# Fifteen pairs and a plain last group: reordering the second layer of a Strassen/Winograd mixture of experts

## The chip, the cores and the metric

The kernel runs on one core of one Trainium2 chip. The metric is the device time in microseconds of one execution; a kernel's time is the median of its runs. Engines are named as in the profile: PE is TensorE (matmul), DVE is VectorE, ACT is ScalarE, POOL is GpSimd, SP is SyncE, whose queue issues all the transfers told of here.

## The reference

```python
def _attn_ref(q, k, v, n_global, n_local):          # q, k, v: 4 x 8 x 768 x 64
    scores = (1 / sqrt(D)) * q @ k^T
    keep = (pos_k < n_global) | ((rel >= 0) & (rel < n_local))   # 8 global, 96 local
    ... # ALiBi-like bias, mask, softmax with + 1e-9 under the sum
    return a @ v

def _moe_ref(x, w_gate, w1, w2):                     # x: 3072 x 512, 8 experts, F = 1024
    P = exp(logits - max)
    for _ in range(8):                               # Sinkhorn
        P /= P.sum(1) + 1e-9;  P /= P.sum(0) + 1e-9;  P *= N / E
    for e in range(8):
        out += P[:, e:e + 1] * (relu(x @ w1[e]) @ w2[e])
```

The attention's output is the input `x` of the mixture; every token goes through every expert.

## The kernel before, in words

Attention runs first, in 8 units of 384 tokens, with a part of expert 0 as filler. Then comes the mixture. All of it is in float32 accuracy: each operand is split into a high part and a rest, and each product is three matmuls (high by rest, rest by high, high by high).

The 3072 tokens are three passes of 1024 (8 tiles of 128). The hidden units that are left are 31 groups (`NG`) of 256 (two tiles of 128): three of expert 0, four of each other expert. The first layer of a group and a pass is Strassen's scheme: seven products m1 to m7, each six matmuls of 128x512, into four PSUM banks a, b, c, d; DVE adds the banks up, and the relu makes four blocks h11, h12, h21, h22.

- **Pass 0** (it works on the last 1024 tokens) prepares each group's weights as it goes: `strassen_stage` loads them (`w1f`, `w2f`) and forms their sums on POOL, `strassen_pair` splits all into high and rest (`split`: ACT casts the high part, POOL subtracts), `spill_weights` writes them to DRAM together with the Winograd sums of w2 (`winograd_blocks`). The second layer of this pass is plain: `second` runs `layer2` tile by tile into `y_ps` and adds into `acc` on DVE. For the first group of expert 1 (g = 3) it scales each of the eight `acc` tiles with the gate first, on ACT (L1175, `first_scaled`). At the head of the pass, `reload_first` fetches the first layer's operands of tokens spilled earlier, the m-operands (`op_m`, tiles named x_... or m_... in the order).
- **Passes 1 and 2** read the prepared weights back (`wb`, a ring of five slots; `load_blocks`, issued two items of the plan ahead). `layer1_scaled` is the first layer; the relu is multiplied by the gate (L750), and the seven operands p1 to p7 of the Winograd scheme are h-blocks or sums of them: POOL forms the sums d7, d5, d6, d4 and all the rests (in an order that is kept), ACT the high parts. `second_layer` runs seven products of six matmuls a group in the order p3, p7, p5, p1, p6, p4, p2, accumulates a chunk of groups in PSUM (`c_acc`) and adds it into `sums` in SBUF: ACT copies it for the first chunk (L1272), DVE adds it for others (L1275). The chunks are (0), (1,2), ..., (29,30). Products p6, p4, p2 of a chunk run after the first half of the next group's first layer.
- **At a pass's end** the last chunk runs whole ("end"). The JOIN additions (L1280, on DVE and two on POOL) make the blocks of the output from the seven sums, `turned` transposes them tile by tile (four 128x128 transposes into one bank `o_t`), and one DVE operation (L1247) adds the pass's seed (expert 0's filler part from attention, `ys`) times the gate; a DMA writes the tile. For pass 1 this is put off until group 0 of pass 2 has its first layer; in pass 2 half of it stands ahead of product p2 and half at the end.

After each product of group 30 in pass 1, `used` reloads that product's operands for pass 2. PE's order is the program's through passes 1 and 2; POOL's is within `layer1_scaled`, SP's and ACT's is at the head of pass 0; elsewhere a scheduler places instructions within each engine. Every DMA of SP waits in its queue for what it needs, and for the landing of the DMA eight before it.

Of the kernel before, what the change touches and what calls it, by code (L numbers as in the profile page):

```python
# [17 lines left out]
P = 128  # L18
# [549 lines left out]
class Moe:  # L568
# [73 lines left out]
    def strassen_pair(self, staged, pool):  # L642

        KH = self.KH
        s, a11, a22, w2f = staged
        w1 = pool.tile([P, 7, 2, KH * P], F32R, name="w1")
        w2 = pool.tile([P, 2, FG, self.DM], F32R, name="w2")

        def cols(a):
            return a.rearrange("p (k c) -> p k c", c=P)  # L650

        self.split(cols(w1[:, 0, 0]), cols(w1[:, 0, 1]), a11)
        self.split(cols(w1[:, 6, 0]), cols(w1[:, 6, 1]), a22)
        self.split(w2[:, 0], w2[:, 1], w2f)
        self.split(w1[:, 1:6, 0], w1[:, 1:6, 1], s.rearrange("p n k c -> p n (k c)"))
        return w1, w2, w2f
# [74 lines left out]

    def layer1_scaled(self, x, blocks, share, full, ops, tmp, ps, tag, waits, used):

# [3 lines left out]
        bank = {n: ps.tile([P, WIDE], F32, name=f"bank_{n}", tag=tag) for n in "cdab"}  # L737
        base = self.block_products(bank, x, blocks)

        def product(m, *args):  # L740
# [13 lines left out]

        def rest(k, src):
            gp(out=ops[k][:, 1], in0=src, in1=ops[k][:, 0], op=ALU.subtract)

# [11 lines left out]
        tt(out=t3, in0=t3, in1=c, op=ALU.subtract)  # L769
        high("p3", h12)  # L770
        gp(out=d7, in0=h12, in1=h22, op=ALU.subtract)
        rest("p3", h12)
        high("p7", d7)
# [7 lines left out]
        if waits:  # L781
            rest("p1", h21)
        product("m7", "a", False, True)
# [8 lines left out]
        gp(out=d4, in0=d6, in1=h11, op=ALU.subtract)  # L792
        rest("p6", d6)
        high("p4", d4)
        high("p2", h11)
        rest("p4", d4)
        rest("p2", h11)

# [116 lines left out]
def pipeline(tc, attention, ident, moe, acc, scratch):  # L915
# [12 lines left out]
    with ExitStack() as top:  # L928
# [154 lines left out]

        reload_first(("m1", "m6", "m3"))
        staged = moe.strassen_stage(*groups[1], stage, sync)
        reload_first(("m4", "m7"))
        for _ in moe.gate(NU - 1, xs[NU - 1], sps, "s", sps, "s"):
# [26 lines left out]
        def spill_weights(g):  # L1114

            w = wts[g]
            t = moe.winograd_blocks(w, w2pool)
            to = w_spill[g] = dram.tile([P, 14, 2, FULL], F32R, name=f"ws{g}")
            dma(to[:, 0:7], w[0])
            dma(to[:, 10], w[1][:, :, 1, 0:FULL])  # L1120
            for d in range(2):
                dma(to[:, 12 + d], w[1][:, :, 0, d * FULL:(d + 1) * FULL])
            dma(to[:, 7:10], t[:, 0:3])
            dma(to[:, 11], t[:, 3])
# [35 lines left out]
        def second(g, hs):  # L1160
            e, b = groups[g][0], passes[0]
            first_scaled = e != 0 and groups[g - 1][0] == 0
            for i in range(2):
                for t in range(WT):
# [6 lines left out]
                    if e == 0:  # L1171
                        nc.vector.tensor_tensor(out=a, in0=y_ps, in1=a, op=ALU.add)
                    else:
                        if first_scaled:
                            nc.scalar.mul(a, a, moe.pm[:, tt, 0:1])  # L1175
                        nc.vector.scalar_tensor_tensor(out=a, in0=y_ps, scalar=moe.pm[:, tt, e:e + 1], in1=a,  # L1176
                                                       op0=ALU.mult, op1=ALU.add)
# [36 lines left out]
        held = [acc[:, j] for j in range(BT)] + [scratch[:, n * WIDE:(n + 1) * WIDE] for n in (2, 3, 4)] + extra  # L1214
        sums = {k: held[2 * n:2 * n + 2] for n, k in enumerate(SECOND_ORDER)}
        moe.pe = attention.pe

        def load_blocks(g, layer, part):
            base, (lo, hi) = 7 * layer, ((0, SPLIT), (SPLIT, 7))[part]
            t = wring.tile([P, SPLIT, 2, FULL], F32R, name="wb")  # L1220
            dma(t[:, 0:hi - lo], w_spill[g][:, base + lo:base + hi])
            for n in range(lo, hi):
                blocks_of[g, layer, n] = t[:, n - lo]

        def first_layer(p, g):
# [8 lines left out]
            return moe.layer1_scaled(ops, lambda i: blocks_of[g, 0, i], share, full, ops_of[g % 2], tmp, mps, "h",  # L1234
                                     g % 2 == 1, used)

        def turned(p, i, seeds):
            outs = sums["p1"] + sums["p6"] if i else list(tmp) + sums["p5"]
            for t in range(WT):
                j = 2 * t + i  # L1240
                tt = passes[p] * BT + j
                o_ps = cps.tile([P, DM], F32, name="o_t", tag="c")
# [4 lines left out]
                nc.vector.scalar_tensor_tensor(out=outs[t], in0=seeds[j], scalar=moe.pm[:, tt, 0:1], in1=o_ps,  # L1247
# [7 lines left out]

        def second_layer(gs, order, ends=False, amid=None):
            begins = gs[0] == 0
            for k in order:
                if amid and k == "p2":
                    amid()  # L1260
                n = SECOND_BLOCKS.index(k)
# [19 lines left out]

        chunks_of = [(0,)] + [(g, g + 1) for g in range(1, NG, 2)]

# [6 lines left out]
        def plan(p):  # L1290

            behind = ()
            for gs in chunks_of:
# [7 lines left out]
                else:  # L1301
                    yield "second", gs, SECOND_ORDER[0:SPLIT]
                    behind = gs

        def loads(what, x, y):
            if what == "first":
                return [(y, 0, 0), (y, 0, 1)]
            if what == "end":
                return [(g, 1, part) for part in range(2) for g in y]
# [3 lines left out]
        for y in loads(*todo[1]):  # L1313
            load_blocks(*y)
        finish = None
        for n, (what, x, y) in enumerate(todo):
            if what == "first":
                rest = first_layer(x, y)
                next(rest)
                if n + 1 < len(todo) and todo[n + 1][2] == SECOND_ORDER[SPLIT:]:  # L1320
                    second_layer(*todo[n + 1][1:])
                next(rest, None)
                if finish:
                    finish()
                    finish = None
            elif what == "second":
                if y != SECOND_ORDER[SPLIT:]:
                    second_layer(x, y)
            elif x + 1 < NB:
                second_layer(y, SECOND_ORDER, True)  # L1330
                seeds = load_seeds(x, [ops_of[y[0] % 2][k][:, s].bitcast(F32) for k in SECOND_ORDER for s in range(2)])

                def finish(p=x, seeds=seeds):
                    for i in (1, 0):
                        turned(p, i, seeds)
            else:
                seeds = load_seeds(x, [a.rearrange("p t k c -> p (t k c)")[:, c:c + WIDE].bitcast(F32)
                                       for m in ("m1", "m6") for a in ops[m] for c in (0, WIDE)])
                second_layer(y, SECOND_ORDER, True, lambda p=x, seeds=seeds: turned(p, 1, seeds))
                turned(x, 0, seeds)  # L1340
            if n + 2 < len(todo):
# [82 lines left out]
```

## Time and profile before

| | |
|---|---|
| median of 3 runs | 2140.99 us (2139.26 to 2141.14) |
| the profiled execution | 2138.77 us, its span 2137.0 us |
| PE busy | 2101.2 us, 98% of the span, 10493 matmuls |
| DVE, ACT, POOL busy | 62%, 34%, 72% |
| data moved | 460.40 MB, mean 215 GB/s |
| granted clock of PE, mean | 0.995 |

A row of the timeline gives the start, the time that the row takes, the engine, the line, what is written and read, how many instructions are merged in it, and in brackets the idle time ahead of it with what ended that. Matmuls overlap, so the pace is read from starts and not from durations.

### The profile page before, as it was taken

The page shows a single profiled execution, that of the slowest core. Times are in us where ns is not written, and L with a number is a line of the kernel's source. Part 1 is how long each engine was busy: PE and PEld are TensorE (multiplying, and loading weights), DVE is VectorE, ACT ScalarE, POOL GpSimd, SP SyncE. Part 2 cuts the span into 40 slices and gives each one's busy share as a digit, 9 for nine tenths or more (in the row PEclk, how much of TensorE's full clock was granted, in tenths as well). Part 3 has the DMA queues.
Part 4 walks back from the last instruction along what each step waited for, and adds up shares of the span by engine and source line. Part 5 has one row for each costly group of instructions (what it writes and reads, how often), then busy time and mean ns, then how long its engine had stood idle before and what let it go on. Part 6 is the DMA issues. An engine that isn't in the chain of part 4 may idle for free. (4 is left out here: it accounts for less than half of the span.)

```text
span 2137.0 us, 30174 instructions
## 1 busy us (share of the span) xinstructions
PE 2101.2 (98%) x10493; PEld 1739.2 (81%) x10493; DVE 1332.1 (62%) x2386; ACT 732.0 (34%) x1498; POOL 1544.2 (72%) x1363
## 2 busy tenths in 40 slices
PE   8999989999999999999999999999899999999997
PEld 6888878888888888878888888888788888888886
DVE  7777657566565665645666556665655666556666
ACT  7778634333233332232222222222232222222221
POOL 5977877777877877457776777767677776777765
PEclk9999999999999999999999999999999999999999
DMA  6777486665666656775565655566965566656553
GB/s 165 214 217 198 146 311 233 235 238 208 240 233 235 241 212 242 246 292 186 203 209 192 217 185 197 204 205 211 354 217 185 194 210 201 208 186 205 205 194 143
DMA packets 235346, 460.40 MB, mean 215 GB/s; under 512 B 106512, under 2 KB 167696, under 8 KB 215472
## 3 DMA queue, kind: packets, MB, share of 16 engines
q1 hardware_dynamic: 235184, 458.37, 63.0%
q8 instruction: 85, 1.39, 0.3%
q14 instruction: 77, 0.63, 0.1%
HBM read 315.38 MB, written 142.93 MB: 214 GB/s over the span
## 5 line engine op out<-in xcount | busy, mean ns | idle before, releaser
L1275 DVE TENSOR_TENSOR early<-early,c_acc 128x512 f32<-128x512 f32 x330 | 225.4, 687 | 187.8 <-PE c_acc L114 187.8
L58 POOL TENSOR_TENSOR early<-full,full 128x512 f32<-128x512 f32 x62 | 80.6, 1300 | 340.6 <-DVE full L750 340.6
L58 POOL TENSOR_TENSOR full<-full,full 128x512 f32<-128x512 f32 x186 | 240.9, 1295 | 0.6 <-PE bank_a L114 0.6
L1176 DVE SCALAR_TENSOR_TENSOR early<-y_ps,pm,early 128x512 f32<-128x512 f32 x224 | 167.8, 749 | 85.0 <-PE y_ps L114 84.7
L114 PE MATMUL bank_c<-x,wb 128*128 128x512 f32 x732 | 186.3, 390 | 3.9 <-issue 2.2
L114 PE MATMUL bank_d<-x,wb 128*128 128x512 f32 x732 | 186.9, 391 | 0.0
L114 PE MATMUL bank_a<-m,wb 128*128 128x512 f32 x732 | 185.8, 389 | 0.0
L114 PEld LDWEIGHTS bank_c<-x,wb 128*128 128x128 f32 x732 | 137.4, 188 | 33.1 <-issue 2.6
L114 PEld LDWEIGHTS bank_d<-x,wb 128*128 128x128 f32 x732 | 138.3, 189 | 28.9
L114 PEld LDWEIGHTS bank_a<-m,wb 128*128 128x128 f32 x732 | 137.6, 188 | 28.6
L114 PE MATMUL y_ps<-w,h_set 128*128 128x512 f32 x672 | 154.8, 389 | 0.0
L114 PE MATMUL y_ps<-w,x 128*128 128x512 f32 x672 | 154.8, 389 | 0.0
L114 PEld LDWEIGHTS y_ps<-w,h_set 128*128 128x128 f32 x672 | 126.0, 188 | 26.1
L114 PEld LDWEIGHTS y_ps<-w,x 128*128 128x128 f32 x672 | 126.0, 188 | 26.1
L114 PE MATMUL c_acc<-x,wb 128*128 128x512 f32 x540 | 137.9, 390 | 2.4 <-DVE early L1275 2.4
L617 POOL TENSOR_TENSOR w<-w1f,w 128x256 fp32r<-128x256 f32 x62 | 44.7, 742 | 129.4 <-ACT w L616 129.4
L761 DVE TENSOR_TENSOR early<-early,bank_d 128x512 f32<-128x512 f32 x62 | 42.7, 688 | 149.0 <-PE bank_d L114 149.0
L114 PEld LDWEIGHTS c_acc<-x,wb 128*128 128x128 f32 x540 | 101.0, 188 | 24.8 <-DVE early L1275 4.1
L639 POOL TENSOR_TENSOR wsum<-w1f 128x256 f32<-128x256 f32 x155 | 109.3, 743 | 13.1 <-DMA w1f<-in_moe_w_dram 13.0
L58 POOL TENSOR_TENSOR x<-full,x 128x512 fp32r<-128x512 f32 x90 | 113.9, 1296 | 0.0
L358 ACT ACTIVATE p_sb<-p_sb,mx 128x256 f32<-128x256 f32 (+1 forms) x192 | 92.5, 483 | 40.8 <-DVE mx L354 40.3
L616 ACT CAST w<-w2f 128x1024 fp32r<-128x1024 f32 x30 | 31.7, 1056 | 209.9 <-issue 163.6
(332 smaller groups left out, 5082.8 us busy)
## 6 DMA issues: line engine op xcount, KB each, us to landing
wb<-ws SPq DMA_DIRECT2D x123, 1024.0 KB, 6.3
wb<-ws SPq DMA_DIRECT2D x123, 768.0 KB, 4.2
ws<-w SPq DMA_DIRECT2D x31, 1792.0 KB, 5.7
ws<-w SPq DMA_DIRECT2D x93, 256.0 KB, 2.5
ws<-w2s SPq DMA_DIRECT2D x31, 768.0 KB, 5.3
w1f<-in_moe_w_dram SPq DMA_DIRECT2D x32, 512.0 KB, 3.8
w2f<-in_moe_w_dram SPq DMA_DIRECT2D x32, 512.0 KB, 4.2
x<-op_m SPq DMA_DIRECT2D x16, 512.0 KB, 9.8
```

Of the source, the lines that this page charges most:

```text
L58: return lambda *args, **kw: self.tc.keep_in_program_order(op(*args, **kw))
L114: return self.tc.keep_in_program_order(self.engine.matmul(*args, **kw))
L358: nc.scalar.activation(out=pv, in_=pv, func=AF.Exp, bias=mx[:, u:u + 1], scale=-1.0, accum_out=sm[:, i, j:j + 1])
L616: self.act.copy(out=hi, in_=full)
L617: self.nc.gpsimd.tensor_tensor(out=lo, in0=full, in1=hi, op=ALU.subtract)
L639: nc.gpsimd.tensor_tensor(out=s[:, n], in0=x, in1=y, op=op)
L761: tt(out=t3, in0=t3, in1=d, op=ALU.subtract)
L1176: nc.vector.scalar_tensor_tensor(out=a, in0=y_ps, scalar=moe.pm[:, tt, e:e + 1], in1=a, op0=ALU.mult, op1=ALU.add)
L1275: nc.vector.tensor_tensor(out=sums[k][q], in0=sums[k][q], in1=bank, op=op)
```

## The change

Six things are changed together.

1. **Pairs.** The chunks are (0,1), (2,3), ..., (28,29), and group 30 stands alone. The pair (28,29) is the "end" with the joins.
2. **A plain last group.** Group 30's first layer follows the joins in program order; it makes no Winograd sums, only high and rest of the four h-blocks. Its w2 is spilled as it is. `turned` then puts four transposes and six plain matmuls of 128x512 into each output bank. Both passes now end in the same way: tiles of i = 1, then of i = 0.
3. **Group 0 of a pass** uses as h-blocks the `sums` of p4, p2 and half of p6, which are not yet in use (`free`), and four of its rests (p1, p6, p4, p2) go to DVE (`begins`). In groups 1 and 30 the rest of p3 stands ahead of d7 (`soon`).
4. **The head of pass 0** asks for all five reloads ahead of group 1's weights.
5. **`strassen_pair`** splits the sums of w1 ahead of w2.
6. **In `second`** of g = 3, the four scalings of i = 1 go to DVE.

```diff
         self.split(cols(w1[:, 6, 0]), cols(w1[:, 6, 1]), a22)
+        self.split(w1[:, 1:6, 0], w1[:, 1:6, 1], s.rearrange("p n k c -> p n (k c)"))
         self.split(w2[:, 0], w2[:, 1], w2f)
-        self.split(w1[:, 1:6, 0], w1[:, 1:6, 1], s.rearrange("p n k c -> p n (k c)"))
...
+        other = tt if begins else gp
...
+        if soon:
+            rest("p3", h12)
+        if plain:
+            high("p7", h22)
+            rest("p7", h22)
+            product("m4", "d", False, True)
+            tt(out=t3, in0=d, in1=t3, op=ALU.add)
+            scaled(h21, d, 0)
+            high("p1", h21)
+            rest("p1", h21)
+            product("m7", "a", False, True)
+            tt(out=a, in0=a, in1=t3, op=ALU.add)
+            scaled(h11, a, 0)
+            high("p2", h11)
+            rest("p2", h11)
+            yield
+            return
...
-        rest("p6", d6)
+        rest("p6", d6, other)
...
-        rest("p4", d4)
-        rest("p2", h11)
+        rest("p4", d4, other)
+        rest("p2", h11, other)
...
-        reload_first(("m1", "m6", "m3"))
+        reload_first(("m1", "m6", "m3", "m4", "m7"))
         staged = moe.strassen_stage(*groups[1], stage, sync)
-        reload_first(("m4", "m7"))
...
+            if g == NG - 1:
+                for f in range(FG):
+                    for s in range(2):
+                        dma(to[:, 7 + 2 * f:9 + 2 * f, s], w[1][:, s, f].rearrange("p (d c) -> p d c", d=2))
+                return
...
+                        if first_scaled and i:
+                            nc.vector.tensor_scalar(out=a, in0=a, scalar1=moe.pm[:, tt, 0:1], scalar2=None, op0=ALU.mult)
+                        elif first_scaled:
-                        if first_scaled:
                             nc.scalar.mul(a, a, moe.pm[:, tt, 0:1])
...
+        free = sums["p4"] + sums["p2"] + sums["p6"][0:1]
...
-                        moe.pe.transpose(out=o_ps[:, at:at + P], in_=sums[k][q][:, t * P:(t + 1) * P], identity=ident)
+                        moe.pe.matmul(o_ps[:, at:at + P], lhsT=sums[k][q][:, cols], rhs=ident, is_transpose=True,
+                                      start=(at == 0), stop=False, skip_group_check=True)
+                for f, h in enumerate((hs["p3"], hs["p7"]) if i else (hs["p2"], hs["p1"])):
+                    for x, (a, b) in enumerate(((0, 1), (1, 0), (0, 0))):
+                        moe.pe.matmul(o_ps, lhsT=h[:, a, cols], rhs=w[:, 2 * f:2 * f + 2, b], start=False,
+                                      stop=(f == 1 and x == 2), skip_group_check=True)
...
-        chunks_of = [(0,)] + [(g, g + 1) for g in range(1, NG, 2)]
+        chunks_of = [(g, g + 1) for g in range(0, NG - 1, 2)]
...
+            yield "plain", p, NG - 1
...
+                seeds = load_seeds(x, [ops_of[1][k][:, s].bitcast(F32) for k in SECOND_ORDER for s in range(2)])
+                next(first_layer(x, y))
+                for i in (1, 0):
+                    turned(x, i, seeds, blocks_of["plain"], ops_of[0])
```

SP's queue at the head of pass 0, before. `x_170`, `x_172`, `m_0_4795`, `m_1_4796` are the operands of m4 and m7, `w1f` and `w2f` the raw weights of a group, `ws` spilled weights, `early<-ys` the seeds of this pass:

```order
L58 DMA w1f<-in_moe_w_dram 128x4x256
L1009 DMA ys_205<-y_sb 128x512
L961 DMA ws_5049<-w_4782 128x2x256 x3
L961 DMA ws_5049<-w_4781 128x3584
L961 DMA xsum<-ws_5049 128x512
L58 DMA early<-ys_204 128x512 x2
L58 DMA early<-ys_205 128x512 x3
L611 DMA w1f<-in_moe_w_dram 128x4x256
L58 DMA w2f<-in_moe_w_dram 128x2x512
L58 DMA x_170<-op_m_195 128x2x256
L58 DMA x_172<-op_m_195 128x2x256
L58 DMA m_0_4795<-op_m_198 128x512
```

The same queue, after:

```order
L58 DMA x_170<-op_m_195 128x2x256
L58 DMA x_172<-op_m_195 128x2x256
L1029 DMA ys_205<-y_sb 128x512
L58 DMA m_0_4795<-op_m_198 128x512
L58 DMA m_1_4796<-op_m_198 128x512
L58 DMA w1f<-in_moe_w_dram 128x4x256
L981 DMA ws_5049<-w_4781 128x3584
L981 DMA ws_5049<-w_4782 128x2x256 x3
L981 DMA xsum<-ws_5049 128x512
L58 DMA early<-ys_204 128x512 x2
L58 DMA early<-ys_205 128x512 x3
L611 DMA w1f<-in_moe_w_dram 128x4x256
L58 DMA w2f<-in_moe_w_dram 128x2x512
```

The four reloads have moved from behind the first two groups' weights to ahead of them.

POOL at the head of pass 1, before: `early` and `full` in the first place of a row are the sums d7, d5, d6, d4, the rows that write p3a to p2a the rests of group 0, and p3b begins group 1:

```order
L58 TENSOR_TENSOR early<-full_10055,full_10054 128x512
L58 TENSOR_TENSOR p3a<-full_10055,p3a 128x512
L58 TENSOR_TENSOR full_10058<-full_10054,full_10056 128x512
L58 TENSOR_TENSOR p7a<-early,p7a 128x512
L58 TENSOR_TENSOR full_10054<-full_10055,full_10058 128x512
L58 TENSOR_TENSOR p5a<-full_10058,p5a 128x512
L58 TENSOR_TENSOR p1a<-full_10056,p1a 128x512
L58 TENSOR_TENSOR full_10055<-full_10054,full_10057 128x512
L58 TENSOR_TENSOR p6a<-full_10054,p6a 128x512
L58 TENSOR_TENSOR p4a<-full_10055,p4a 128x512
L58 TENSOR_TENSOR p2a<-full_10057,p2a 128x512
```

The same engine, after:

```order
L58 TENSOR_TENSOR early<-extra_10050,early 128x512
L58 TENSOR_TENSOR p3a<-extra_10050,p3a 128x512
L58 TENSOR_TENSOR early<-early,extra_10051 128x512
L58 TENSOR_TENSOR p7a<-early,p7a 128x512
L58 TENSOR_TENSOR early<-extra_10050,early 128x512
L58 TENSOR_TENSOR p5a<-early,p5a 128x512
L58 TENSOR_TENSOR extra_10050<-early,extra_10052 128x512
L58 TENSOR_TENSOR p3b<-full_10046,p3b 128x512
L58 TENSOR_TENSOR early<-full_10046,full_10045 128x512
L58 TENSOR_TENSOR full_10049<-full_10045,full_10047 128x512
L58 TENSOR_TENSOR p7b<-early,p7b 128x512
```

Group 0 has seven rows where it had eleven, and p3's rest of group 1 stands ahead of its d7.

PE at the end of the last pass, before. `c_acc<-x_170,wb` and `c_acc<-p4a,wb` are the two groups of product p4, `x_172` and `p2a` those of p2, `o_t<-ident` transposes:

```order
L114 MATMUL c_acc<-x_170,wb 128x512 x6
L114 MATMUL c_acc<-p4a,wb 128x512 x6
L117 MATMUL o_t<-ident,early 128x128 x16
L114 MATMUL c_acc<-x_172,wb 128x512 x6
L114 MATMUL c_acc<-p2a,wb 128x512 x6
L117 MATMUL o_t<-ident,extra_10060 128x128
```

The same engine, after: the first two output tiles, behind the last product of group 30's first layer (`bank_a`, m7):

```order
L114 MATMUL bank_a<-m_1_4796,wb 128x512
L114 MATMUL bank_a<-m_0_4795,wb 128x512 x2
L114 MATMUL o_t<-ident,early 128x128 x4
L114 MATMUL o_t<-wb,p3a 128x512 x3
L114 MATMUL o_t<-wb,p7a 128x512 x3
L114 MATMUL o_t<-ident,early 128x128 x4
L114 MATMUL o_t<-wb,p3a 128x512 x3
L114 MATMUL o_t<-wb,p7a 128x512 x3
```

The transposes that stood in two blocks, one ahead of p2 and one at the end, now alternate tile by tile with six matmuls, behind a whole first layer.

More of the change, by code (lines that the diff above doesn't have):

```diff
@@ L730, in block_products, with layer1_scaled @@
         return product
-    def layer1_scaled(self, x, blocks, share, full, ops, tmp, ps, tag, waits, used):
+    def layer1_scaled(self, x, blocks, share, full, ops, tmp, ps, tag, waits, used, begins, soon, plain):
         nc = self.nc
@@ L753, in high, with rest @@
             nc.scalar.copy(out=ops[k][:, 0], in_=src)
-        def rest(k, src):
-            gp(out=ops[k][:, 1], in0=src, in1=ops[k][:, 0], op=ALU.subtract)
+        def rest(k, src, engine=gp):
+            engine(out=ops[k][:, 1], in0=src, in1=ops[k][:, 0], op=ALU.subtract)
         product("m3", "c", True, False)
@@ L770, in layer1_scaled @@
         high("p3", h12)
+        if soon:
[15 more added lines that the diff above has]
+            return
         gp(out=d7, in0=h12, in1=h22, op=ALU.subtract)
-        rest("p3", h12)
+        if not soon:
+            rest("p3", h12)
         high("p7", d7)
@@ L781, in layer1_scaled @@
         if waits:
-            rest("p1", h21)
+            rest("p1", h21, other)
         product("m7", "a", False, True)
@@ L1116, in spill_weights @@
             w = wts[g]
-            t = moe.winograd_blocks(w, w2pool)
+            if g < NG - 1:
+                t = moe.winograd_blocks(w, w2pool)
             to = w_spill[g] = dram.tile([P, 14, 2, FULL], F32R, name=f"ws{g}")
             dma(to[:, 0:7], w[0])
+            if g == NG - 1:
[3 more added lines that the diff above has]
+                return
             dma(to[:, 10], w[1][:, :, 1, 0:FULL])
@@ L1221, in load_blocks @@
             dma(t[:, 0:hi - lo], w_spill[g][:, base + lo:base + hi])
+            if layer and g == NG - 1:
+                blocks_of["plain"] = t
             for n in range(lo, hi):
@@ L1232, in used, with turned @@
                     reload(p + 1, (m,))
[L1234 to L1238, printed above, removed]
+            return moe.layer1_scaled(ops, lambda i: blocks_of[g, 0, i], share, free if g == 0 else full, ops_of[g % 2], tmp, mps, "h",
+                                     g % 2 == 0, used, g == 0, g in (1, NG - 1), g == NG - 1)
+        def turned(p, i, seeds, w, hs):
+            outs = sums["p1"] + sums["p6"] if i else sums["p7"] + sums["p5"]
             for t in range(WT):
@@ L1241, in turned @@
                 tt = passes[p] * BT + j
+                cols = slice(t * P, (t + 1) * P)
                 o_ps = cps.tile([P, DM], F32, name="o_t", tag="c")
@@ L1254, in pipeline, with second_layer @@
                        ("p4", "p4", "p6", ALU.add))}
-        def second_layer(gs, order, ends=False, amid=None):
+        def second_layer(gs, order, ends=False):
             begins = gs[0] == 0
             for k in order:
-                if amid and k == "p2":
-                    amid()
                 n = SECOND_BLOCKS.index(k)
@@ L1307, in loads @@
                 return [(y, 0, 0), (y, 0, 1)]
+            if what == "plain":
+                return [(y, 0, 0), (y, 0, 1), (y, 1, 0)]
             if what == "end":
@@ L1314, in pipeline @@
             load_blocks(*y)
-        finish = None
         for n, (what, x, y) in enumerate(todo):
@@ L1319, in pipeline @@
                 next(rest)
-                if n + 1 < len(todo) and todo[n + 1][2] == SECOND_ORDER[SPLIT:]:
+                if todo[n + 1][2] == SECOND_ORDER[SPLIT:]:
                     second_layer(*todo[n + 1][1:])
                 next(rest, None)
-                if finish:
-                    finish()
-                    finish = None
             elif what == "second":
@@ L1328, in pipeline @@
                     second_layer(x, y)
-            elif x + 1 < NB:
+            elif what == "end":
                 second_layer(y, SECOND_ORDER, True)
[L1331 to L1335, printed above, removed]
-            else:
[L1337 to L1340, printed above, removed]
+            else:
+                seeds = load_seeds(x, [ops_of[1][k][:, s].bitcast(F32) for k in SECOND_ORDER for s in range(2)])
+                next(first_layer(x, y))
+                for i in (1, 0):
+                    turned(x, i, seeds, blocks_of["plain"], ops_of[0])
             if n + 2 < len(todo):
```

## The prediction

> **What bounds the kernel now.** I read the busy times first, then who waited for whom on TensorE (PE), then the places of these waits in order of time.
>
> The page's first section, busy time and share of the span:
>
> ```profile
> PE 2101.2 (98%) x10493; PEld 1739.2 (81%) x10493; DVE 1332.1 (62%) x2386; ACT 732.0 (34%) x1498; POOL 1544.2 (72%) x1363
> ```
>
> PE is the bound. Of the span of 2137.0 us it is idle for 35.8 us, so the change can win only there, in the few stretches in which PE runs at a lower clock, and behind its last instruction. Who PE waited for (total, times, longest):
>
> ```profile
> PE o_t L117 <- DVE early L1280: 4.3, 2, 2.9
> PE bank_d L698 <- DMA x<-op_m: 4.2, 1, 4.2
> PE c_acc L114 <- DVE early L1275: 2.4, 4, 0.7
> PE bank_c L114 <- issue: 2.2, 1, 2.2
> PE c_acc L114 <- POOL p3a L58: 2.1, 1, 2.1
> PE bank_c L114 <- DMA wb<-ws: 1.7, 1, 1.7
> PE c_ps L908 <- DVE pm L906: 1.4, 1, 1.4
> PE bank_c L114 <- ACT early L814: 1.1, 1, 1.1
> PE c_acc L114 <- POOL p5a L58: 0.8, 1, 0.8
> PE c_acc L114 <- POOL p7a L58: 0.8, 1, 0.8
> ```
>
> These ten rows lie in five places, which I name H0 (head of pass 0: op_m, pm), G3 (L814), H1 (head of pass 1: p3a, p7a, p5a), T1 (turn from pass 1 to 2: issue, wb, half of the L1275 waits) and T2 (end: L1280, the other half of L1275). Three stretches of 5 us have a lowered clock (busy us of PE, PEld, DVE, ACT, POOL with counts, then PEclk, DMA share, GB/s), each behind long waits:
>
> ```profile
> 285.00:290.00 5.00, 3.20 (x8) 2.52 (x9) 0.23 (x1) 2.20 (x2) 3.58 (x2) 0.50 0.52 180
> 1525.00:1530.00 5.00, 3.97 (x12) 3.15 (x13) 1.60 (x3) 0.62 (x1) 1.16 (x1) 0.71 1.01 418
> 2120.00:2125.00 5.00, 3.52 (x18) 3.47 (x18) 5.00 (x9) 0.00 (x0) 0.00 (x0) 0.66 0.14 52
> ```
>
> The pace, from two neighbouring products of six matmuls at T1:
>
> ```profile
> 1506.33 1.52 PE L114 MATMUL c_acc<-x,wb 128*128 128x512 f32 x6
> 1507.69 1.52 PE L114 MATMUL c_acc<-p6a,wb 128*128 128x512 f32 x6
> ```
>
> Starts 1.36 us apart: 0.227 us for a 128x512 matmul. A group of 42 is 9.52 us.
>
> **H0, operands ahead of weights.** PE at the head, then SP's queue, then ACT:
>
> ```profile
> 277.27 0.50 PE L698 MATMUL bank_c<-x,w 128*128 128x512 f32 x1
> 293.75 0.98 PE L844 MATMUL y_ps<-w,h_set 128*128 128x512 f32 x3
> ...
> 278.76 0.50 SPq L58 DMA_DIRECT2D w2f<-in_moe_w_dram  x1
> 279.37 1.35 SPq L58 DMA_DIRECT2D x<-op_m  x2
> ...
> 285.29 1.04 ACT L58 CAST w<-w2f 128x1024 fp32r<-128x1024 f32 x1 [5.18 <-DMA w2f<-in_moe_w_dram]
> 286.24 1.25 ACT L58 CAST w<-wsum 128x1280 fp32r<-128x1280 f32 x1
> ```
>
> The 16.48 us hold 30 matmuls (6.8) and two small gate products (0.6): 9.1 us are lost, to the waits of 1.4 and 4.2 and to the lowered clock. m4's operands are issued behind w2f at 279.37, and PE has them only at 286.8. The change puts their four loads (2 MB) ahead of all of group 1's weights, so m5, m4, m7 run back to back, then the gate product and m3, m2 of group 1: five products and 0.6 us, from 277.27 to about 284.9. Late next is bank_a for m1: the relu of the bank_c result stands on ACT behind the cast of w2f, and w2f is still issued at about 279. If it lands as before (285.3), cast, ACT's half of the relu (0.6) and DVE's (0.7) free bank_a's chain at about 287.7; ACT's cast of wsum (1.25) and one more relu then let y_ps start near 289.7. If it lands 2 us earlier, since 2 MB no longer compete, y_ps starts near 288. Before, with m1 of group 1 added to be comparable, it is 293.75 + 1.36 = 295.1. Gain 5 to 7; a wait of some 3 us that lowers the clock again takes about 2 back. I take 5.0, ends 3 and 7. The reordered split costs nothing by itself: the same casts, wsum's first, and its input is ready sooner.
>
> On the clock, the waits of 1.72 and 2.17 us at T1, neither long, already go with 0.71. The Trainium skill ("TensorE: Matmul & The Clock Gate", Part 1: The HAM clock gate) has the clock halve after an idle window of about 3.4 us and come back after about 3.4 busy ones. The 4.2 us wait with 0.50 behind it agrees; the 0.71 shows that two shorter waits do it too. By the page's rule alone H0 would keep its full clock and gain near 6.
>
> **G3, four scalings from ACT to DVE.**
>
> ```profile
> 355.83 5.01 ACT L1175 ACTIVATE early<-early,pm 128x512 f32<-128x512 f32 x8
> 360.75 0.57 ACT L814 COPY early<-bank_c 128x512 f32<-128x512 f32 x1
> ```
>
> PE waits 1.1 us for that copy. Four scalings end at about 358.3, the copy by 358.9, ahead of PE's need at 360.1. DVE gains four instructions (0.7 each) ahead of its own additions; these are paced by PE's products. Gain 1.3 with the restart, ends 0 (DVE becomes late) and 1.3.
>
> **H1, group 0 paired.** PE's first second-layer product, and POOL's first and last of group 0's eleven operations:
>
> ```profile
> 931.39 1.67 PE L114 MATMUL c_acc<-p3a,wb 128*128 128x512 f32 x6 [2.10 <-POOL p3a L58]
> ...
> 927.41 1.29 POOL L58 TENSOR_TENSOR early<-full,full 128x512 f32<-128x512 f32 x1 [23.90 <-DVE full L750]
> 941.26 1.28 POOL L58 TENSOR_TENSOR p2a<-full,p2a 128x512 fp32r<-128x512 f32 x1
> ```
>
> PE finishes group 0's first layer at 929.1 to 929.3 (931.39 less its wait) and then asks for each of POOL's results 1.36 us apart, while POOL makes one in 1.25: three waits, 3.7 us, with restarts of 0.15 to 0.3 us each 4.6 lost. With (0,1) a pair, group 1's first layer (9.52 us) runs in that time; the second layer starts at 938.65. POOL has 7 operations for group 0 (four rests moved to DVE) and p3, d7, d5, p7 of group 1. The tightest is p7 of group 1: its cast stands on ACT behind an eviction (0.6) of the first bank of p3, which is full near 940.7; cast 941.9, POOL's rest 943.2, against PE's need at 938.65 + 3 x 1.36 = 942.73. Left 0.6; ends 0 and 2.5 (DVE's four rests next to POOL, below). Gain 4.0, ends 2.1 and 4.6.
>
> The moved rests are DVE additions of two SBUF inputs beside POOL. At T1 the same kind costs:
>
> ```profile
> 1504.41 4.63 DVE L1280 TENSOR_TENSOR early<-early 128x512 f32<-128x512 f32 x3
> 1519.49 1.87 DVE L1275 TENSOR_TENSOR extra<-extra,c_acc 128x512 f32<-128x512 f32 x3
> ```
>
> 1.54 us each beside a busy POOL against 0.62 (the second row has PSUM as an input and no POOL beside it). So four rests are 2.5 us alone and 6.2 at worst beside POOL, and POOL is slowed with them; that is where 2.5 comes from. The Trainium skill ("SBUF — State Buffer", Terms) says the two share a port pair held for a whole instruction, so the loser blocks; the 1.54 agrees, and by that rule H1 gains 2.1 and not 4.0.
>
> **T1, the turn.** PE, and SP's issue of pass 2's first weights:
>
> ```profile
> 1518.16 1.61 PE L114 MATMUL bank_c<-x,wb 128*128 128x512 f32 x6 [1.72 <-DMA wb<-ws]
> 1526.03 2.00 PE L114 MATMUL bank_c<-x,wb 128*128 128x512 f32 x6 [2.17 <-issue]
> 1531.83 1.91 PE L117 MATMUL o_t<-ident,early 128*128 128x128 f32 x16
> 1533.58 0.38 PE L117 MATMUL o_t<-ident,extra 128*128 128x128 f32 x2
> 1536.39 0.27 PE L117 MATMUL o_t<-ident,extra 128*128 128x128 f32 x1
> 1536.71 1.63 PE L114 MATMUL c_acc<-p3a,wb 128*128 128x512 f32 x6
> ...
> 1506.50 0.42 SPq L961 DMA_DIRECT2D wb<-ws  x1
> ```
>
> From 1506.33 to 1536.71 are 30.38 us with 78 matmuls (17.7) and 32 transposes of 0.109 (16 in 1.75 us; 3.5): 9.2 lost. 1.7 are the two waits for evictions behind the joins (0.48 and 0.72 with restarts), about 6 the weights of pass 2, issued at 1506.50 behind 14 reloads (waits of 1.72 and 2.17, and the clock). In the changed kernel the reloads follow the products of group 30, after the second layer. Counted from that start, PE has 9.52 of first layer and 14.4 of plain work ahead of pass 2: its weights, ahead of the reloads in the queue, are wanted at about 25 us, m7's operands at 33. The queue holds 1.75 MB of weights, 7.2 of reloads, 1.75 more of weights and 0.5 of gate rows, 11.2 MB, at the 418 GB/s of the window row above 27 us, at 400 28: in time for all but perhaps the gate rows (wanted at 31.7).
>
> Left: 1.7 for the evictions; 0.85 for the last rests ahead of the first plain product; 0.6 at pass 2's head as at H1: 3.2. Added: 6 matmuls (48 plain for 42), 1.36; and the switches. Going from transposes to matmuls costs 0.32 - 0.11 = 0.2 us at 1536.39, of which 0.08 a wait; I take 0.15 for each of eight tiles, 1.2, ends 0 and 0.25 each (2.0). That the four transposes and six products share a bank makes PE wait for nothing but the bank's last reader four tiles back. DVE has one L1247-like operation (0.74) a tile in 1.8 us. Gain 9.2 - 3.2 - 1.4 - 1.2 = 3.4, ends -1 (the backlog) and 5.5.
>
> **T2, the end.**
>
> ```profile
> 2109.42 1.52 PE L114 MATMUL c_acc<-x,wb 128*128 128x512 f32 x6
> 2119.68 0.33 PE L117 MATMUL o_t<-ident,early 128*128 128x128 f32 x1 [2.85 <-DVE early L1280]
> 2129.88 0.27 PE L117 MATMUL o_t<-ident,extra 128*128 128x128 f32 x1
> 2128.88 2.72 DVE L1247 SCALAR_TENSOR_TENSOR early<-m,pm,o_t 128x512 f32<-128x512 f32 x4 [0.64 <-PE o_t L117]
> ```
>
> From 2109.42 to 2137.0 are 27.58 us: three products of the last pair (8.2), 32 transposes, 1.7 of eviction waits, 2.85 and 1.48 for the joins, the clock, and 5.4 from DVE's last operation (2131.60) to the end. To compare, I add a first layer and a second layer of one group (9.52 each), which the changed kernel runs, or replaces, behind that point: 46.6. After: three products 8.2, evictions 1.7, first layer of group 30 9.5, with the joins under it (at T1 DVE was done with joins and evictions at 1521.36, 4.9 us after PE's last second-layer product, 1518.16 less its wait; that is inside 9.5), rests 0.85, eight tiles of 4 x 0.109 + 6 x 0.227 = 1.80, 14.4, and from the last matmul one DVE operation and 5.4, 6.4: 41.1, with switches 42.3. Gain 4.4, ends 3 and 5.6.
>
> **The sum.** 5.0 + 1.3 + 4.0 + 3.4 + 4.4 = 18.1 us off. The fourteen DVE and ACT evictions fewer a pass lie beside PE and count nothing. The profiled run took 2138.77 (1.8 outside the span) and goes to 2120.7; the median of the three runs, 2140.99, is 2.2 above it. I forecast 2122 for the median. The sum of the ends is 7 to 24.
>
> **Rivals.**
> 1. *The backlog moves.* One mechanism against the change: the 11.2 MB of the turn no longer fit. Against: PE has 25 us, not 10, before it needs the first of them. For: each DMA of SP waits for the one eight before it, so a late one delays all behind. At half the 418 GB/s of the window row the 11.2 MB take 54 us, the gate rows come 22 late, T1's gain and the other 14.7 are gone, and the time is about 2147. It decides from about 220 GB/s, where 19 us are lost.
> 2. *H0 only moves its wait.* w2f and the clock take the 5 back, and DVE's shared port costs H1 two: gain 11, 2129. For: the wait for w2f of 5.18 on ACT was there already, hidden behind the operands.
> 3. *No wait is left.* w2f early, free switches, no rest late: gain 24, 2116. For: the 0.85, the 0.6 and H0's wait rest on landings and casts that may come sooner than taken.
> 4. *The plain tiles do not run as priced,* a wait between transposes and products of 0.5 us in each of sixteen: 5.6 more than taken, gain 12.5, 2128. The 0.2 us at 1536.71 speaks against it, though there the banks differ.
>
> **How the numbers follow.** A change below 0.2% (4.3 us) cannot be told from none here. Forecast (gain 15 to 22) 0.50; rival 2 0.16; rival 4 0.12; rival 3 0.12; several terms at their low ends, within 4.3 us, 0.06; rival 1 0.04. Faster 0.90, same 0.06, slower 0.04. The range takes in rivals 2 to 4 with 2 us for the runs: 2114 to 2132.
>
> **What would show it.** H0: no wait for op_m, one of 1 to 3.5 us at m1 of group 1. G3: no wait on the copy of bank_c near 360. H1: at most one wait of about 0.6 for p7 of group 1. T1: no wait for wb; tiles 1.8 to 2.0 us apart. T2: no wait for the joins. Wrong would be a PE wait for x, m or wb at pass 2's head, or tiles over 2.2 us apart.

## The result, and the profile after

The changed kernel took 2125.09 us (median of 4 runs, 2124.13 to 2126.08) against 2141.06 us before (4 runs, 2139.26 to 2141.40): a ratio of 0.9927 with a 95% interval of 0.9910 to 0.9944, 16.0 us faster, 3 us above the forecast and inside its range. The profiled execution took 2126.08 us with a span of 2124.3.

Busy times of the changed kernel:

```profile
PE 2101.6 (99%) x10505; PEld 1739.4 (82%) x10505; DVE 1326.6 (62%) x2370; ACT 724.9 (34%) x1487; POOL 1515.4 (71%) x1336
```

Who PE waited for (total us, times, longest):

```profile
PE bank_a L698 <- DVE h_set L706: 4.2, 1, 4.2
PE c_acc L114 <- DVE early L1309: 2.4, 4, 0.7
PE c_acc L114 <- POOL p7b L58: 2.4, 2, 1.3
PE bank_c L698 <- ACT early L834: 0.8, 1, 0.8
PE o_t L114 <- POOL p3a L58: 0.6, 2, 0.3
PE o_t L114 <- POOL p7a L58: 0.6, 2, 0.3
```

PE's busy time is the same to 0.4 us, though it has twelve matmuls more: the span lost idle time, 35.8 us before and 22.7 now. The waits for joins (o_t behind L1280), for op_m and for wb are gone, and so are those of the second layer for p3a, p7a and p5a at pass 1's head. The evictions behind joins wait as before (2.4 in four). New are the wait of 4.2 us for a relu, those for p7b, one of 0.8 for ACT's copy of bank_c (L834) and four of 0.3 for rests in the plain tiles.

Set against each other where PE stands at the same work, the two first profiles give:

| place | forecast, us | measured, us | how read |
|---|---|---|---|
| H0, head of pass 0 | 5.0 | 0.5 | PE was 0.56 late on entering and 0.10 late behind it |
| G3 | 1.3 | 1.4 | 0.10 late ahead of it, 1.31 early behind it |
| H1, head of pass 1 | 4.0 | 2.8 | 4.6 lost before; now 1.9, as four products (5.44) take 7.30 from p3a's start to p5a's |
| T1, turn and pass 2's head | 3.4 | 2.8 | 4.7 at the turn, 1.9 given back at the head |
| T2, the end | 4.4 | 5.8 | 46.6 before, as the forecast counts it; 40.8 now, from the start of p6 (2083.51) to the end |
| sum | 18.1 | 13.3 | less 0.56 in attention: 12.7, the difference of the two profiled executions |

The medians differ by 3.3 us more than the two profiled executions. Experiment e13 below shows one source: the wait in H0 of the kernel before differs between executions, and the one profiled first had the shorter of the two that were profiled.

**H0.** PE of the changed kernel; then SP, then ACT:

```profile
286.07 0.39 PE L700 MATMUL bank_d<-x,w 128*128 128x512 f32 x1
290.63 0.80 PE L698 MATMUL bank_a<-m,w 128*128 128x512 f32 x1 [4.18 <-DVE h_set L706]
...
280.58 0.70 SPq L611 DMA_DIRECT2D w1f<-in_moe_w_dram  x1
281.37 0.46 SPq L58 DMA_DIRECT2D w2f<-in_moe_w_dram  x1
...
287.09 0.71 ACT L616 CAST w<-w1f 128x256 fp32r<-128x256 f32 x2 [3.92 <-DMA w1f<-in_moe_w_dram]
288.31 1.04 ACT L58 CAST w<-w2f 128x1024 fp32r<-128x1024 f32 x1 [0.52 <-DMA w2f<-in_moe_w_dram]
289.27 0.59 ACT L705 ACTIVATE h_set<-bank_c 128x512 fp32r<-128x512 f32 x1
```

m5, m4 and m7 do run back to back. But the relu of bank_c (289.27) stands on ACT behind two casts that wait for transfers: group 2's w1f and group 1's w2f, which go out at 280.58 and 281.37 instead of 278.33 and 278.76. PE waits 4.18 us for bank_a, as long as it had waited for m4's operands. The clock falls behind this wait too, and the 14 matmuls that start from 290.63 on take 6.15 us instead of 3.17:

```profile
290.00:295.00 5.00, 4.37 (x10) 3.47 (x11) 3.93 (x10) 3.18 (x4) 5.00 (x5) 0.50 0.55 187
```

**G3.** ACT of the changed kernel, then DVE:

```profile
355.94 2.56 ACT L1202 ACTIVATE early<-early,pm 128x512 f32<-128x512 f32 x4
358.40 0.57 ACT L834 COPY early<-bank_c 128x512 f32<-128x512 f32 x1
...
355.55 4.79 DVE L1200 TENSOR_SCALAR early<-early,pm 128x512 f32<-128x512 f32 x4
```

The copy is done at 358.97, where the forecast had 358.9, and PE does not wait for it. DVE's four scalings took 1.2 us each and not the 0.7 that the forecast had for them; they cost PE nothing.

**H1.** POOL of the changed kernel, DVE's last rest, ACT and PE:

```profile
931.72 1.74 POOL L58 TENSOR_TENSOR p7a<-early,p7a 128x512 fp32r<-128x512 f32 x1
934.67 1.29 POOL L58 TENSOR_TENSOR p5a<-early,p5a 128x512 fp32r<-128x512 f32 x1
941.83 1.27 POOL L58 TENSOR_TENSOR p7b<-early,p7b 128x512 fp32r<-128x512 f32 x1
...
938.89 1.83 DVE L758 TENSOR_TENSOR p4a<-extra,p4a 128x512 fp32r<-128x512 f32 x1
...
940.46 0.63 ACT L755 CAST p7b<-early 128x512 fp32r<-128x512 f32 x1
...
937.34 1.52 PE L114 MATMUL c_acc<-p3a,wb 128*128 128x512 f32 x6
943.15 1.65 PE L114 MATMUL c_acc<-p7b,wb 128*128 128x512 f32 x6 [1.16 <-POOL p7b L58]
944.64 1.52 PE L114 MATMUL c_acc<-p5a,wb 128*128 128x512 f32 x6
```

The long wait is where it was forecast, at p7 of group 1, and twice as long: 1.16 (1.3 with restart) for 0.6; the rest of the 1.9 is a start 0.28 late at p3 of group 1 and two restarts of 0.13. Four of POOL's operations up to this rest took 1.74 us beside DVE's rests, which like the joins have two inputs in SBUF; the others took 1.29.

**The plain tiles.** PE at the turn; then the start of the end's p6 on PE and the last operation of DVE:

```profile
1503.82 0.73 PE L114 MATMUL o_t<-wb,p3a 128*128 128x512 f32 x2 [0.28 <-POOL p3a L58]
1505.63 0.60 PE L114 MATMUL o_t<-ident,early 128*128 128x128 f32 x4
1507.45 0.60 PE L114 MATMUL o_t<-ident,early 128*128 128x128 f32 x4
1518.44 1.54 PE L114 MATMUL bank_c<-x,wb 128*128 128x512 f32 x6
...
2083.51 1.52 PE L114 MATMUL c_acc<-p6a,wb 128*128 128x512 f32 x6
2118.95 0.75 DVE L1283 SCALAR_TENSOR_TENSOR early<-p1b,pm,o_t 128x512 f32<-128x512 f32 x1 [1.08 <-PE o_t L114]
```

Tiles start 1.82 us apart, and the sum of their instructions was 1.80: the switch that was priced at 0.15 costs 0.03. Pass 2's first product starts at 1518.44 with no wait for its weights or operands. The end's tiles run at the same pace; DVE is done at 2119.70, 4.6 us ahead of the end of the span, where it was 5.4 before.

### The profile page after: what moved, and what is told of

It reads as the page before. It is cut to its first block, busy times and chain, and to the rows that moved or that the text cites. A ratio compares the mean times of both kernels' runs of the same rounds, so it can differ in the third digit from the quotient of the medians.

```text
span 2124.3 us, 30115 instructions
## 1 busy us (share of the span) xinstructions
PE 2101.6 (99%) x10505; PEld 1739.4 (82%) x10505; DVE 1326.6 (62%) x2370; ACT 724.9 (34%) x1487; POOL 1515.4 (71%) x1336
## 4 chain that ended last, share of the span: by engine, by line
PE 91%; POOL 3%; issue 2%; DVE 2%; DMA 1%; ACT 1%; SPq 0%; DVEq 0%; POOLq 0%; ACTq 0%
PE c_acc L114 25%; PE y_ps L114 16%; PE bank_c L114 11%; PE bank_d L114 11%; PE bank_a L114 11%; PE bank_b L114 5%; PE o_ps L114 2%; PE t_ps L117 2%; PE s_ps L114 2%; PE h_ps L114 1%; PE tp L117 1%; PE o_t L114 1%; PE y_ps L864 1%; PE y_ps L866 1%; PE y_ps L865 1%
## 5 line engine op out<-in xcount | busy, mean ns | idle before, releaser
L1309 DVE TENSOR_TENSOR early<-early,c_acc 128x512 f32<-128x512 f32 x308 | 210.3, 687 | 174.7 <-PE c_acc L114 174.7
L58 POOL TENSOR_TENSOR early<-full,full 128x512 f32<-128x512 f32 x58 | 76.0, 1310 | 290.9 <-DVE full L752 290.9
L58 POOL TENSOR_TENSOR full<-full,full 128x512 f32<-128x512 f32 x174 | 225.8, 1298 | 0.0
L755 ACT CAST x<-full 128x512 fp32r<-128x512 f32 x90 | 56.0, 622 | 160.8 <-POOL full L58 136.1
```

Of the source, the lines that this page charges most:

```text
L58: return lambda *args, **kw: self.tc.keep_in_program_order(op(*args, **kw))
L755: nc.scalar.copy(out=ops[k][:, 0], in_=src)
L1309: nc.vector.tensor_tensor(out=sums[k][q], in0=sums[k][q], in1=bank, op=op)
```

## Experiments

"The relus first" (e3) is the kernel that later ones build on, since its runs lie closer together. The experiments ran in three comparisons, each on another chip and with the kernel before beside it: e1 to e4 (2140.42 before), e5 to e8 (2139.71) and the others (2140.47). These times before differ by up to 0.8 us, so a difference of about 1 us across comparisons says little by itself, and the waits in the profiles are read beside it.

**e1, both head edits undone, and e4, the changed kernel again.**

```diff
-        reload_first(("m1", "m6", "m3", "m4", "m7"))
+        reload_first(("m1", "m6", "m3"))
         staged = moe.strassen_stage(*groups[1], stage, sync)
+        reload_first(("m4", "m7"))
...
-        self.split(w1[:, 1:6, 0], w1[:, 1:6, 1], s.rearrange("p n k c -> p n (k c)"))
         self.split(w2[:, 0], w2[:, 1], w2f)
+        self.split(w1[:, 1:6, 0], w1[:, 1:6, 1], s.rearrange("p n k c -> p n (k c)"))
```

> The changed kernel with both edits of the head of pass 0 undone: m4's and m7's operands again behind group 1's weights, w2 split ahead of w1's sums. Theory (the head's gain was spent: the weights go out 2.6 to 5 us later behind the reloads, and PE waits 4.2 us for the relu that stands on ACT behind the casts of these weights): the same as the changed kernel within 1.5 us, about 2125, with the wait of about 4 us for op_m back in H0. Rival (the profiled execution was an unlucky one; the head is worth its 5 us in the median): about 2130.

> The changed kernel once more, on the same chip as the others, unchanged. Both theories: 2125 within 1 us. For the size of the wait in H0: if it is set by when a transfer of 0.5 MB lands, it varies between executions (1 to 4.5 us); if by the order on ACT and SP alone, it is again 4.2 within 0.3.

e1 took 2127.78 (2127.16 to 2130.59), e4 2125.28 (2123.60 to 2125.64). The two head edits are worth 2.5 us, half of the 5.0 forecast: neither expectation of e1 had it. Against the kernel before in this comparison the change is worth 15.1 us, beside 16.0 in the first. e4's wait at bank_a was 3.6 us against 4.18 in the first profile, so landings do move it, by less than the bounds that were expected.

**e2, only the split's order undone.**

```diff
+        self.split(w2[:, 0], w2[:, 1], w2f)
         self.split(w1[:, 1:6, 0], w1[:, 1:6, 1], s.rearrange("p n k c -> p n (k c)"))
-        self.split(w2[:, 0], w2[:, 1], w2f)
```

> The changed kernel with only the order inside the weights' split undone (w2 ahead of w1's sums), the reloads still ahead. Theory: ACT casts group 1's w2f, which lands at about 288, ahead of the sums; their rests follow on POOL (2.9 us), so m2 of group 1 waits until about 293 instead of m1 until 290.6: about 2128, with one PE wait of 6 us or more in H0. Rival (the split order costs and brings nothing, since both casts wait for landings alike): 2125.

2125.65, with a wide spread (2123.36 to 2128.16): the same median as the changed kernel. Its wait in the profile, the fastest of its runs, is at m2 of group 1, as the theory had it, but shorter:

```profile
PE bank_d L698 <- ACT w L58: 3.5, 1, 3.5
```

The split's order chooses which product waits for ACT, not whether one does. By this median it is worth nothing that can be told from the spread.

**e3, the relus ahead of the casts.** Group 1's w2 is split behind the first layer of group 0, and ACT's order is kept until group 1 is through.

```diff
-        wts[1] = moe.strassen_pair(staged, wpools[1])
-        moe.act = nc.scalar
+        wts[1] = moe.strassen_pair(staged, wpools[1], True)     # True: w2 not split here
...
             hs = moe.layer1_strassen(ops, wts[g], h_sets[g % 2], tmp, mps, "h", g == 0, beat)
+            if g == 0:
+                moe.split(wts[1][1][:, 0], wts[1][1][:, 1], wts[1][2])
...
+            if g == 1:
+                moe.act = nc.scalar
```

> The changed kernel, with ACT's relus of group 0 of pass 0 put ahead of the cast of group 1's w2f and of group 2's weights. Theory (the 4.2 us wait at m1 of group 1 is the relu behind these casts, and the half clock behind it is its consequence): the wait for the relu and the half clock go, 6 to 7 us less, about 2118 to 2119. Rival (the next thing is late as well: group 2's weights, which are now cast later, or the seeds): 2 to 3 us less at most, 2122, with a new wait between 285 and 312 us.

2119.04 (2118.77 to 2119.74), 0.9903 (0.9888 to 0.9918) of the time before: 6.2 us less than the changed kernel beside it (e4). ACT, and the two windows in which the clock had been 0.99 and 0.50:

```profile
282.85 0.60 ACT L58 ACTIVATE h_set<-bank_c 128x512 fp32r<-128x512 f32 x1 [2.43 <-DVE early L849]
287.16 1.05 ACT L58 CAST w<-w2f 128x1024 fp32r<-128x1024 f32 x1 [2.74 <-DMA w2f<-in_moe_w_dram]
...
285.00:290.00 5.00, 5.00 (x24) 4.13 (x23) 2.11 (x7) 2.48 (x3) 4.04 (x6) 1.00 0.94 393
290.00:295.00 5.00, 5.00 (x24) 4.17 (x23) 4.61 (x12) 0.60 (x1) 4.92 (x4) 1.00 0.49 165
```

w2f lands hardly earlier (cast at 287.16), and PE is busy all through: nothing but ACT's order held it up.

**e5, the reloads between w1 and w2** (on the changed kernel; `between` is called in `stage_pair` behind w1's DMA).

```diff
-        reload_first(("m1", "m6", "m3", "m4", "m7"))
-        staged = moe.strassen_stage(*groups[1], stage, sync)
+        reload_first(("m1", "m6", "m3"))
+        staged = moe.strassen_stage(*groups[1], stage, sync, lambda: reload_first(("m4", "m7")))
```

> The changed kernel, with the reloads of m4 and m7 between group 1's w1 and its w2 (w1, m4, m7, w2) instead of ahead of both. Theory (the relu behind the casts on ACT sets PE's wait; the weights' issue only shifts it): w1's sums are ready some 5 us earlier, but the casts that wait are those of group 2's w1f and group 1's w2f, issued behind the same seeds: wait of 2 to 4 us at m1 of group 1 is still there, 2123 to 2125. Rival (the weights were late because they stood behind the reloads, and that is the whole loss): the wait goes, 2119.

2127.27 (2125.11 to 2127.55), 0.9938 (0.9924 to 0.9952) of the time before, where e4 had 0.9929: about 2 us slower than the changed kernel, which neither had. Group 1's sums are cast at 274.70, but group 2's w1f lands later still (cast at 288.05), and with it the relu:

```profile
PE bank_a L700 <- DVE h_set L708: 5.8, 1, 5.8
```

That group 1's w1 stood behind the reloads was not the cause. Its w2 stands behind the reloads here too, so e5 says nothing of that.

**e12, the head alone.** The kernel before with e3's head and nothing else of the change (the diffs of e1 reversed, and e3's).

> The kernel before, with only the head of pass 0 changed: reloads ahead of group 1's weights, the sums' split first, and the relus ahead of the casts. Theory: the head's whole loss (9.1 us in the trace before, of which about 1 stays) is to be had by these three together, and the scalings of g = 3 stand behind the copy here, so G3's 1.3 goes too: 2130 to 2131.5. Rival (part of the loss in the head is the seeds' or gate's, which appears once the operands are there): 2134.

2130.33 (2128.99 to 2131.03), 0.9950 (0.9936 to 0.9963): 10.1 us off. In its profile H0 has one wait of 0.5 us, and G3 none, as the eight scalings stand behind the copy here. So nearly all of the loss in the head was to be had; the change took about a quarter of it.

**e13, the kernel before once more.**

> The kernel before once more. All theories: the same as before within 0.5 us; the profile shows how much the wait for m4's operands differs between executions (4.2 in the first; if landings vary as in the changed kernel, 3 to 6).

2139.94, a ratio of 0.9998 (0.9989 to 1.0007). Its profile:

```profile
PE bank_d L698 <- DMA x<-op_m: 6.0, 1, 6.0
```

The wait for m4's operands was 4.2 in the profile that the forecast was made from and is 6.0 here, and the span is 2139.4 instead of 2137.0. H0 of the kernel before costs 9.1 to 11.2 us (PE is 2.7 us later behind it than in the first profile, and had entered it 0.6 later), so the 0.5 of the table becomes 2.6 with this execution, near e1's 2.5. It was the slowest of the eleven (2141.17), so the 2.1 us are the upper end of what this explains of the 3.3 between medians and profiles. For the rest, the execution of the changed kernel that was profiled was the slowest of its four, 1.0 above their median.

**e8, all scalings on ACT** (on e3).

```diff
-                        if first_scaled and i:
-                            nc.vector.tensor_scalar(out=a, in0=a, scalar1=moe.pm[:, tt, 0:1], scalar2=None, op0=ALU.mult)
-                        elif first_scaled:
+                        if first_scaled:
```

> The kernel with the relus first (2119.0), with all eight scalings of g = 3 on ACT as before the change. Theory: the wait of 1.1 us for ACT's copy of bank_c comes back near 350 us, 1.3 to 1.4 more: 2120.4. Rival (ACT's copy is late by less, since the head now runs earlier): 2119 to 2119.5.

2118.68 (2118.33 to 2118.99), 0.9900 of the time before against e3's 0.9903: no cost, the rival's number for another reason. With e3's head ACT has the copy of bank_c at 348.44 and all eight scalings behind it, from 351.20. What cost 1.3 us was the place of the scalings ahead of the copy; how many there are matters only in that place.

**e6, three rests back on POOL, later** (on e3).

```diff
-        rest("p6", d6, other)
...
-        rest("p4", d4, other)
-        rest("p2", h11, other)
+        if begins:       # group 0: kept, and run on POOL behind group 1's operations
+            self.late = [lambda k=k, s=s: rest(k, s) for k, s in (("p6", d6), ("p4", d4), ("p2", h11))]
+            return
...
+        for late in self.late:
+            late()
```

> The kernel with the relus first (2119.0), with three of group 0's four moved rests (p6, p4, p2) back on POOL, but behind all of group 1's operations. Theory (five of POOL's operations took 1.74 instead of 1.29 us beside DVE's rests and joins, and these 2.2 us are p7's wait of 1.2 at both heads): POOL's operations at the heads go back to 1.29, p7's wait falls to 0.4 or less and that of p3 to nothing, about 2 us less over both heads: 2117. Rival (p7's wait is set by its cast on ACT behind an eviction): the wait stays at 1.2, 2119.

2117.72 (2117.26 to 2120.01): 1.3 us less than e3 and 1.0 less than e8 beside it, between the two and within the spread. The profile is plainer: from p3a's start to p5a's, four products, PE takes 6.76 and 6.09 us at the two heads, where e8 takes 7.42 and 7.41, so 2.0 us are won there. POOL's operations are back at 1.29 but for one at each head, and p7b of pass 1's head now waits on ACT:

```profile
932.63 1.29 POOL L58 TENSOR_TENSOR full<-full,full 128x512 f32<-128x512 f32 x1
934.65 1.27 POOL L58 TENSOR_TENSOR p7b<-early,p7b 128x512 fp32r<-128x512 f32 x1 [0.73 <-ACT p7b L757]
```

Both theories hold one behind the other: POOL's slowing made p7 late, and at pass 1 the cast, which stands behind an eviction and another cast, does once the slowing is gone (1.0 left at pass 1, 0.35 at pass 2). The slowing was four operations at each head, not the five of the expectation.

**e7, the joins spread** (on e3).

```diff
-        JOIN = {"p5": (("p3", "p3", "p5", ALU.add), ("p4", "p7", "p4", ALU.subtract), ("p5", "p5", "p7", ALU.add)),
-                "p1": (("p2", "p2", "p1", ALU.add),),
-                "p6": (("p6", "p6", "p1", ALU.add), ("p5", "p5", "p6", ALU.add), ("p3", "p3", "p6", ALU.add),
-                       ("p4", "p4", "p6", ALU.add))}
+        JOIN = {"p6": (("p3", "p3", "p5", ALU.add), ("p6", "p6", "p1", ALU.add)),
+                "p4": (("p5", "p5", "p7", ALU.add), ("p5", "p5", "p6", ALU.add)),
+                "p2": (("p3", "p3", "p6", ALU.add),),
+                "late": (("p4", "p7", "p4", ALU.subtract), ("p4", "p4", "p6", ALU.add), ("p2", "p2", "p1", ALU.add))}
```

> The kernel with the relus first (2119.0), with all joins on DVE, none ahead of p1's and p6's evictions, and those of p4 and p2 behind group 30's first layer. Theory (DVE's joins took 1.54 instead of 0.62 us since POOL was at work, and made two evictions and later two rests late): the waits of 0.48 and 0.72 for evictions and of 0.3 for the rests of p3 and p7 go, 2.6 us with restarts in each pass: 2114. Rival (DVE has the same work before the plain tiles, so what the evictions gain the rests lose): 2117 to 2119, with longer waits at the first tile.

2117.70 (2117.49 to 2118.40): 1.3 us less than e3 and 1.0 less than e8, the rival's number but not its cause, since the rests wait no longer than before. DVE at the turn:

```profile
1473.96 4.61 DVE L1299 TENSOR_TENSOR early<-early 128x512 f32<-128x512 f32 x3
1481.48 2.49 DVE L1299 TENSOR_TENSOR early<-early 128x512 f32<-128x512 f32 x4
```

The first three joins were still put beside POOL's last rests (1.54 each), and the wait of 0.48 stayed; the next four, with POOL idle, took 0.62, and the wait of 0.72 fell to 0.22. The rests of p3 and p7 still wait 0.2 to 0.3. Over both ends the waits for evictions fall from 2.4 to 1.4 us.

**e9, e6 and e7 together.**

> Both e6 and e7 on the kernel with the relus first. They act at different places (heads of passes 1 and 2; ends of both passes), so their gains of 1.3 each should add: 2116.4. Rival (POOL at pass 2's head or DVE at the turn is shared between them): 2117.5.

2115.84 (2115.31 to 2116.64), 0.9886 (0.9871 to 0.9901) of the time before: faster than the kernel before by 24.6 us and than the changed one by 9.3 us. Against e3 it is 3.2 us less, so the two gains add; the waits for p7b (1.7 for 2.4) and for evictions (1.4 for 2.4) both fall.

**e10, the pairs without the plain group** (on the kernel before; two lines that go by a group's parity are turned with it).

```diff
-        chunks_of = [(0,)] + [(g, g + 1) for g in range(1, NG, 2)]
+        chunks_of = [(g, g + 1) for g in range(0, NG - 1, 2)] + [(NG - 1,)]
```

> The kernel before, with only the chunks changed: (0,1), (2,3), ..., (28,29), and then (30) alone as the Winograd end with its joins; no plain group, h-blocks and rests as before. Theory (the pairs pay at pass 1's head, the plain group pays at the two ends): 3 us less at the head, but the joins now stand in products of 1.36 instead of 2.72 us and DVE has them all still to do when PE is through: 3 to 5 us more at each end, 2143 to 2147, slower than before. Rival (the end's order does not matter, the pairs are the change): 2137.

2145.78 (2143.36 to 2149.72), 1.0025 (1.0015 to 1.0034): slower by 5.3 us. Waits of PE:

```profile
PE c_acc L114 <- POOL p3b L58: 6.3, 2, 4.9
PE o_t L117 <- DVE early L1280: 6.1, 2, 4.8
```

The time lies in the theory's range, but in part by luck, for the places do not come out as it has them. At pass 1's head it expected 3 us less. POOL still has all of group 0's eleven operations ahead of group 1's rests, PE waits 4.9 us for p3b, and the next two products start 2.73 and 2.43 us apart instead of 1.36: 7.6 us are lost there, where it was 4.6. At the ends it expected 3 to 5 us more each. By the same count (products and transposes at their pace, the rest lost) the end of pass 2 costs 0.9 more, and the turn with pass 2's head 1.1. The wait for the joins is there as the theory had it, 6.1 where it was 4.3. The pairs alone bring nothing at the head, and they leave the wait for the joins, which is gone with the plain group.

## Why the prediction was right, and where it was not

The direction of the time and the sign of each place were right; the sum of 18.1 was measured as 16.0 in the medians and 12.7 in the first profiles. That the medians come so near is in part luck: H0 gave half of its 5.0 or less, T2 gave more than its upper end, and the kernel before loses more in H0 than the execution that the forecast was made from. By its own sum the forecast would be 2122.9 (2140.99 less 18.1), not 2122.

- **H0 failed, 5.0 for 0.5 in the first profiles and 2.5 in the medians.** The step that failed is "late next is bank_a for m1". It named the right relu and the right engine, and priced the wait at w2f's landing of 285.3 or sooner. The landing was near 288.3 (the cast waits for it until then): w2f goes out 2.6 us later than before, of which PE's 0.56 on entering is a part, and the cast of group 2's w1f, which the step left out, stands on ACT ahead of the relu as well. The first spill of group 1's weights also goes out while w2f is under way (284.02); that it slows the landing is not shown. e3 shows that ACT's order was the cause of PE's wait, e5 that the place of group 1's w1 behind the reloads was not. For a lowered clock the step took 2 us; it cost 3.0. Second, "the reordered split costs nothing" was short by 0.84: the copy of bank_c stands behind the sums' cast now.
- **The clock.** The wait of 4.18 us had 0.50 behind it. The Trainium skill ("TensorE: Matmul & The Clock Gate", Part 1: The HAM clock gate) has the clock halve after an idle window of about 3.4 us, and this agrees; behind e3's wait of 0.5 the clock stayed at 1.00.
- **G3** was right (1.4 for 1.3), though DVE's scalings took 1.2 us each for 0.7. e8 and e12 show that a change of order alone would do it: there all eight scalings stand on ACT behind the copy.
- **H1** is 2.8 for 4.0, inside its ends. The place was right; the term that was mis-sized is POOL beside DVE's rests, which the forecast had only as the low end of 2.1. The Trainium skill ("SBUF — State Buffer", Terms) has the loser of the shared port block; here both engines lengthen, POOL from 1.29 to 1.74 and DVE to as much as 1.83. e6 agrees that the sharing costs: with most of it gone, 2.0 us come back at the two heads.
- **T1** is 2.8 for 3.4. The evictions' 1.7 (1.8 measured) and the backlog's absence were right. The switches cost 0.25 for 1.2, the rests 1.1 for 0.85, and pass 2's head 2.0 for 0.6: the same POOL term as at H1. No run separates what the reloads' new place and the plain group each give at the turn.
- **T2** is 5.8 for 4.4, above its upper end of 5.6: the joins are hidden by group 30's first layer as worked out, of the switches' 1.2 only some 0.2 came, and the span ends 4.6 us behind DVE's last operation instead of 5.4. e10, the pairs without the plain group, keeps the wait for the joins.
- **Rivals.** Of the four, 2 came nearest: H0 did move its wait, and DVE beside POOL cost H1 one us; the gain was 16 and not 11, since T2 gave more and the kernel before loses more in H0 than its first profile showed. 1 did not occur (no wait for weights or operands at pass 2's head), nor 3, nor 4. The 2147 of rival 1 counts T1's gain twice: 22 us late on a gain of 18.1 is 3.9 us more than before, about 2145.

## What to carry to other kernels

Before an operand is moved forward in a queue, look at the in-order engine that frees the next buffer: a relu behind casts that wait for transfers cost as much as the operand had. Work of the last stage that only adds up results goes under an independent stretch of PE work, and not into products too short to cover it. A second engine's help with additions in SBUF is worth counting at the slowed rate of both.

## What the runs showed of the hardware

A wait for one transfer differs between executions of the same program: 4.2 and 6.0 us for m4's operands, 3.6 and 4.2 for the relu behind w2f. One profile of this kernel therefore fixes such a term to about 2 us, and medians can differ from it by as much. Four transposes and six matmuls that add into one bank run 1.82 us apart for a sum of 1.80. A DVE addition with two SBUF inputs took 0.62 us with POOL idle and 1.54 beside it, and POOL's 1.29 became 1.74: three joins in 4.61 us against four in 2.49 (e7).
